# Attention scores with the memory keys stationary in 64x32 tiles and the queries moving, copied out and transposed back on TensorE

## The chip, the cores and the metric

The kernel runs on one core of a Trainium2 chip. The core has a matrix engine (PE, which loads a stationary operand, LDWEIGHTS, and then streams a moving operand through it, MATMUL), a vector engine (DVE), a scalar engine (ACT), a general engine (POOL) and a queue engine that issues the DMAs (SP). Matmul results land in PSUM and are read from there by DVE and ACT; everything else lies in SBUF. Each engine executes its own instructions in the order in which they were written and waits on semaphores for the others. The metric is the device time of one execution in microseconds.

## The reference

For each of 8 batches and 8 heads, 576 tokens of 64 dimensions are condensed into 32 memory slots, the tokens attend to the slots, and two feed-forward blocks follow:

```
a      = softmax over tokens of phi                 # [576, 32] per head
k_m    = a^T k ;  v_m = a^T v                       # [32, 64] per head
scores = q k_m^T / sqrt(64)                         # [576, 32] per head
attn   = softmax over the 32 slots of scores
x      = attn v_m                                   # heads side by side: [576, 512]
u      = x + (x^T U V)^T ;  y = u + relu(u w1) w2   # 512 -> 2048 -> 512
h      = relu(y w_in) ; gate the two halves, mix tokens with w_spatial ; out = gated w_out
```

The change is in the line `scores`.

## The kernel before

A generator, `att(b)`, prepares the attention of batch b while the matrix products of batch b-1 run: its pieces end in `yield`, and the product phases call it piece by piece. Batch 0 has a routine of its own (`first`), which the change leaves as it is, so the changed code runs 7 times, for batches 1 to 7. For batch 1 it is interleaved with the products of batch 0 (`mm<-gw,w2r` in f32 at L794), for batch 2 with the f16 products at L854, and for batches 3 to 7 with those of `st_phase` (L899, L910, L933), five times in the same order. Where the code is not inside a manual schedule, a scheduler places each instruction by its own model; the PE queue then holds what it holds in that order.

In `att` the steps around the change are: the condensed keys and values `nkv` (L592), two PE transposes of them into `tps` (L598), the copies out of `tps` (L601 by ACT for the keys, L606 by DVE for the values), a scale by way of `absmax`, `bmax_a` and `bmax_b` (the last one a small matmul at L159), and then the scores in three groups of token tiles, (0, 1), (2, 3) and (4,), of 128 tokens each and 64 in the last. For each group there is a bank of PSUM `sps`. Per token tile four matmuls (L629) hold 128 tokens of a pair of heads of `q` stationary and stream 64 columns of `kmt`, a block-diagonal tile of the keys of both heads (its other half is zero from the start). Each matmul of f32 operands is shown in the trace as two LDWEIGHTS and two MATMULs. DVE takes the maximum over the 32 slots (L633) and subtracts it (L636), ACT takes the exponential (L638), and in the next piece DVE sums and divides (L642 to L646), and ACT and DVE split the result into two f16 halves `ahl` (L650, L651). All of `ahl` is then multiplied with `u3h` (L660, ten matmuls, the last two on token tile 4).

The queries come in by `load_q` (L277): token tile s lies in one of two buffers `qt`, so tile s+2 can be loaded only once the scores of tile s have been computed. The SP queue issues these loads in order with all others. Token tile 4 of batches 3 to 7 is loaded early into a piece of `gw`. PSUM tiles named `at` share three banks, `mm` tiles five. `tmp` tiles share five buffers.

Of the kernel before, what the change touches and what calls it, by code (L numbers as in the profile page):

```python
# [12 lines left out]
ACTF = mybir.ActivationFunctionType  # L13
# [17 lines left out]
def mixer_kernel(  # L31
# [34 lines left out]
    def t1k():  # L66
        return tp.tile([128, 256], F32, tag="t1k", name="t1k", bufs=2)
# [81 lines left out]
    def bmax_a(am, n=128):  # L149
        e = tiny(1, I32)  # L150
        dve.tensor_single_scalar(e[:n], am[:n].bitcast(I32), EXP_MASK, op=ALU.bitwise_and)
        dg = tp.tile([128, 128], BF16, tag="dgb", name="dgb", bufs=3)
        dve.tensor_scalar(out=dg[:n, :n], in0=identb[:n, :n], scalar1=e[:n].bitcast(F32),
                          scalar2=None, op0=ALU.mult)
        return dg
# [112 lines left out]
    def rows(s):  # L268
        return 128 if s < 4 else 64
# [279 lines left out]
    def att(b):  # L549
# [46 lines left out]
        tps = at_tile()  # L596
        for g in range(2):
            pe.transpose(tps[:, g * 128:(g + 1) * 128], nkv[:, g * 128:(g + 1) * 128], ident)  # L598
        for e_ in range(2):
            r0 = slice(64 * e_, 64 * e_ + 64)  # L600
            act.activation(kmt[r0, :, e_, :],  # L601
                           tps[r0, e_ * 128:(e_ + 1) * 128].rearrange("p (q m) -> p q m", m=M), func=ACTF.Copy)
        vmt32 = a["vmt32"] = t1k()[:, 0:128]
        for e_ in range(2):
            r0 = slice(64 - 64 * e_, 128 - 64 * e_)
            dve.tensor_copy(vmt32[r0], tps[r0, e_ * 128:(e_ + 1) * 128])  # L606
        av = tiny()
        absmax(av, vmt32)
        dg = bmax_a(av)
        yield  # L610
        yield
        mv, rv, sv = sc[:, 4:5], sc[:, 5:6], sc[:, 6:7]
        bmax_b(dg, mv)
# [5 lines left out]
                                 op0=ALU.mult, op1=ALU.subtract)  # L619
        ahl = tp.tile([128, NST, 2, 256], F16, tag="pa", name="ahl")  # L620
        pool.memset(ahl[64:128, 4], 0.0)
        for grp in ((0, 1), (2, 3), (4,)):
            r = rows(grp[0])
            n = len(grp)
            sps = at_tile()
            for i, s in enumerate(grp):
                o4 = sps[:r, i * 256:(i + 1) * 256].rearrange("p (e q m) -> p e q m", e=2, m=M)
                for p in range(4):
                    pe.matmul(o4[:, :, p, :], a["q"][s][:, p, :r], kmt[:, p], start=True, stop=True)  # L629
                load_q(b, s + 2)  # L630
            sv3 = sps[:r, 0:n * 256].rearrange("p (h m) -> p h m", m=M)
            mxs = tiny(16)
            dve.tensor_reduce(out=mxs[:r, :n * 8], in_=sv3, axis=AX.X, op=ALU.max)  # L633
# [3 lines left out]
                              in1=mxs[:r, :n * 8].unsqueeze(2).to_broadcast([r, n * 8, M]), op=ALU.subtract)  # L637
            act.activation(ex[:r, 0:n * 256], ex[:r, 0:n * 256], func=ACTF.Exp, scale=0.125)  # L638
            yield
            yield  # L640
            sm = tiny(16)
            dve.tensor_reduce(out=sm[:r, :n * 8], in_=ex3, axis=AX.X, op=ALU.add)  # L642
# [1076 lines left out]
```

## Time and profile before

| | us |
|---|---|
| median of 3 runs | 1139.64 (1138.35 to 1140.41) |
| the profiled execution | 1138.26 |
| its span, first to last instruction | 1136.5 |
| PE busy | 1119.4 (98%) |
| DVE busy | 843.1 (74%) |
| ACT busy | 609.3 (54%) |
| L629, 280 records of score matmuls, busy | 32.2 (28.8 + 3.4) |

The span leaves 1.8 us of the execution outside it. An instruction is named by line, engine, operation and `output<-inputs`; a duration of PE is the time from entering to leaving the array, so that neighbours overlap, and what a group of matmuls costs is read from where the next group starts. "Idle before" is time in which the engine had nothing running, with the engine and tile that ended it.

### The profile page before, as it was taken

To read this page: it belongs to the slowest core of one execution; us is meant where nothing else is said; L and a number is where in the kernel's file an instruction comes from. 1 tells how busy PE (TensorE), PEld (TensorE's weight loads), DVE (VectorE), ACT (ScalarE), POOL (GpSimd) and SP (SyncE) were. 2 spreads that over 40 slices of the span, in tenths; PEclk is the share of its full clock that TensorE was granted. 3 is DMA by queue.
4 is the path that set the end of the run, shared out by engine and by line. 5 is a ranking of instruction groups with operands and counts; after the bars stand their busy time and mean duration, and the time that the engine had idled before them with its cause. 6 is when DMAs were issued, how large, how long until landed. Compare 5 with 4: busy or idle time off the path is not lost.

```text
span 1136.5 us, 28937 instructions
## 1 busy us (share of the span) xinstructions
PE 1119.4 (98%) x12015; PEld 884.4 (78%) x12015; DVE 843.1 (74%) x2217; ACT 609.3 (54%) x1308; POOL 90.5 (8%) x316
## 2 busy tenths in 40 slices
PE   8899999999999999999999999999999999999998
PEld 6566776777667997789867997779967898679966
DVE  6767688878786786868776787867868687866854
ACT  4768765746446354564365454563555543653543
POOL 3101011000010001100010000100011000100000
PEclk9999999999999999999999999999999999999999
DMA  9869741341526231441316213261304303130201
GB/s 357 315 259 348 263 173 59 117 147 39 184 79 208 72 127 42 151 147 60 146 59 218 87 36 148 93 206 60 144 25 157 125 20 128 44 111 2 110 19 43
DMA packets 54852, 145.69 MB, mean 128 GB/s; under 512 B 7808, under 2 KB 37248, under 8 KB 43584
## 3 DMA queue, kind: packets, MB, share of 16 engines
q1 hardware_dynamic: 54208, 143.16, 35.8%
q8 instruction: 94, 1.54, 0.6%
q10 hardware_dynamic: 512, 0.67, 0.2%
q14 instruction: 38, 0.31, 0.1%
HBM read 120.32 MB, written 23.49 MB: 127 GB/s over the span
## 4 chain that ended last, share of the span: by engine, by line
PE 85%; DVE 7%; ACT 4%; DMA 2%; issue 1%; POOL 1%; ACTq 0%; POOLq 0%; DVEq 0%
PE mm L899 23%; PE mm L933 13%; PE mm L1198 10%; PE mm L1228 8%; PE mm L1157 6%; PE mm L1086 5%; PE mm L794 4%; PE at L629 2%; PE mm L854 2%; PE at L735 2%; PE at L578 2%; PE mm L771 1%; PE mm L817 1%; PE mm L910 1%; DMA wsr<-w2d 1%
## 5 line engine op out<-in xcount | busy, mean ns | idle before, releaser
L899 PE MATMUL mm<-gw,w2r 128*128 128x144 f16 x2304 | 168.8, 226 | 0.0
L899 PEld LDWEIGHTS <-w2r 128*128 128x128 f16 x2304 | 152.4, 98 | 5.0
L933 PE MATMUL mm<-apr,z 128*128 128x288 f16 x1152 | 155.1, 286 | 0.0
L933 PEld LDWEIGHTS <-z 128*128 128x128 f16 x1152 | 109.7, 98 | 28.3 <-issue 2.0
L899 PE MATMUL mm<-gw,wa 128*128 128x144 f16 x1728 | 127.9, 226 | 0.0
L937 ACT ACTIVATE wsr<-mm 128x288 f32<-128x288 f32 x192 | 78.3, 408 | 86.2 <-DVE gw L921 42.8
L1198 PE MATMUL mm<-wsr,gw 128*128 128x288 f16 x896 | 114.3, 286 | 1.7 <-ACT gw L1161 1.6
L899 PEld LDWEIGHTS <-wa 128*128 128x128 f16 x1728 | 111.3, 98 | 3.5 <-issue 1.0
L1198 PEld LDWEIGHTS <-gw 128*128 128x128 f16 x896 | 85.6, 98 | 32.1 <-issue 9.7
L1157 PE MATMUL mm<-yhl,gw 128*128 128x288 f16 x768 | 99.4, 286 | 0.0
L1228 PE MATMUL mm<-ghl,wa 128*128 128x288 f16 x768 | 97.8, 286 | 0.0
L1228 PEld LDWEIGHTS <-wa 128*128 128x128 f16 x768 | 74.4, 98 | 22.8 <-issue 3.8
L1157 PEld LDWEIGHTS <-gw 128*128 128x128 f16 x768 | 73.4, 98 | 18.6 <-issue 0.6
L939 DVE TENSOR_TENSOR wsr<-wsr 128x288 f32<-128x288 f32 x96 | 44.0, 458 | 56.7 <-ACT wsr L937 56.7
L1086 PE MATMUL mm<-gw,yhl 128*128 128x512 f16 x384 | 85.5, 379 | 0.0
L921 DVE TENSOR_TENSOR gw<-wsr,gw 128x720 f16<-128x720 f32 x96 | 85.5, 900 | 0.0
L1213 ACT ACTIVATE ghl<-gw,ysc 128x288 f16<-128x288 f32 x64 | 34.2, 535 | 83.2 <-DVE gw L1212 83.2
L920 ACT ACTIVATE gw<-wsr 128x720 f16<-128x720 f32 x96 | 76.4, 796 | 0.5
L1086 PEld LDWEIGHTS <-yhl 128*128 128x128 f16 x384 | 37.0, 98 | 41.7
L794 PE MATMUL mm<-gw,w2r 128*128 128x288 f32 x256 | 65.9, 409 | 0.0
L1092 DVE BATCH_NORM_STATS2 tiny<-tmp 128x6 f32<-128x512 f32 (+1 forms) x40 | 25.6, 639 | 46.9 <-ACT tmp L1090 46.8
L794 PEld LDWEIGHTS mm<-gw,w2r 128*128 128x128 f32 x256 | 47.5, 190 | 15.1 <-issue 1.5
(309 smaller groups left out, 1867.2 us busy)
## 6 DMA issues: line engine op xcount, KB each, us to landing
wa<-w1d SPq DMA_DIRECT2D x22, 1024.0 KB, 5.0
kvt<-in_kv_dram SPq DMA_DIRECT2D x28, 516.0 KB, 5.0
gw<-wid SPq DMA_DIRECT2D x12, 1024.0 KB, 7.4
wsr<-wsd SPq DMA_DIRECT2D x7, 1440.0 KB, 6.3
out_dram<-tmp SPq DMA_DIRECT2D x64, 144.0 KB, 2.3
qt<-in_qT_dram SPq DMA_DIRECT2D x28, 256.0 KB, 3.7
gw<-in_w_dram SPq DMA_DIRECT2D x6, 1024.0 KB, 8.2
wa<-wod SPq DMA_DIRECT2D x6, 1024.0 KB, 4.8
```

The source lines that it names most:

```text
L794: pe.matmul(ps, w2r[:, f, d * 128:(d + 1) * 128], AT[0]["g"][:, f, :], start=False, stop=(f == 15))
L899: pe.matmul(ps[:, dd * QH:(dd + 1) * QH], w(c, dd, 1 - x), gs[:, m, c, y, :], start=(first and c == 0 and dd == 0 and i == 0), stop=(end a ...
L920: act.activation(h, X[:, 3:8], func=ACTF.Copy)
L921: dve.tensor_tensor(out=gs[:, 2:7, c, 1, :], in0=X[:, 3:8], in1=h, op=ALU.subtract)
L933: pe.matmul(ps, a["z"][:, k, x, f * 128:(f + 1) * 128], a["apr"][:, k, y, sl], start=(i == 0), stop=(i == 5))
L937: act.activation(o, pair(ps), func=ACTF.Relu, scale=CG)
L939: dve.tensor_tensor(out=X[:, 4:6], in0=X[:, 2:4], in1=X[:, 1:3], op=ALU.subtract)
L1086: pe.matmul(ps, yhl[:, k, x, s * 128:(s + 1) * 128], wih[:, k, 0, 1 - y, :], start=(i == 0), stop=(i == 11))
L1157: pe.matmul(ps, wih[:, k, 1, 1 - x, d * 128:(d + 1) * 128], a["yhl"][:, k, y, sl], start=(i == 0), stop=(i == 11))
L1198: pe.matmul(pss[d], vn[:, s, x if s < 4 else 0, ds], wsh[:, s, th, 1 - y, :], start=(s == 0 and i == 0), stop=(s == 4 and i == 1))
L1213: act.activation(ghl[:, d, 0, sl], u2, func=ACTF.Identity, scale=sgt)
L1228: pe.matmul(ps, (wo0 if b else woh)[:, k, 1 - x, d * 128:(d + 1) * 128], a["ghl"][:, k, y, sl], start=(i == 0), stop=(i == 11))
```

## The change

For each pair of heads the keys now lie plain in `kT` (64 rows of one head, 32 columns a pair), stationary, and the 128 tokens of `q` move. Eight matmuls per token tile, one for each head, go to eight different 64x32 tiles of the array (row half by `e_`, column quarter by `p`) and write two PSUM tiles, one for each `e_`, of 128 partitions (4 heads by 32 slots) by tokens. Two ACT copies bring them into a `tmp` tile `sT`, and PE transposes give the old layout back in `sps`. The matmuls of a group stand one or more pieces ahead of the transposes.

```diff
--- before.py
+++ after.py
@@ -596,18 +596,38 @@
         tps = at_tile()
         for g in range(2):
             pe.transpose(tps[:, g * 128:(g + 1) * 128], nkv[:, g * 128:(g + 1) * 128], ident)
+        vk = t1k()
+        vmt32, kT = vk[:, 0:128], vk[:, 128:256]
+        a["vmt32"] = vmt32
         for e_ in range(2):
             r0 = slice(64 * e_, 64 * e_ + 64)
-            act.activation(kmt[r0, :, e_, :],
-                           tps[r0, e_ * 128:(e_ + 1) * 128].rearrange("p (q m) -> p q m", m=M), func=ACTF.Copy)
-        vmt32 = a["vmt32"] = t1k()[:, 0:128]
+            act.activation(kT[r0], tps[r0, e_ * 128:(e_ + 1) * 128], func=ACTF.Copy)
         for e_ in range(2):
             r0 = slice(64 - 64 * e_, 128 - 64 * e_)
             dve.tensor_copy(vmt32[r0], tps[r0, e_ * 128:(e_ + 1) * 128])
         av = tiny()
         absmax(av, vmt32)
         dg = bmax_a(av)
+        G = ((0, 1), (2, 3), (4,))
+        sT = {}
+
+        def scores(i):
+            r = rows(G[i][0])
+            n = r * len(G[i])
+            ps = [at_tile() for e_ in range(2)]
+            for k, s in enumerate(G[i]):
+                for p in range(4):
+                    for e_ in range(2):
+                        r0 = slice(64 * e_, 64 * e_ + 64)
+                        pe.matmul(ps[e_][32 * p:32 * p + 32, k * r:(k + 1) * r], kT[r0, 32 * p:32 * p + 32],
+                                  a["q"][s][r0, p, :r], start=True, stop=True)
+                load_q(b, s + 2)
+            sT[i] = tmp()
+            for e_ in range(2):
+                act.activation(sT[i][:, e_ * 256:e_ * 256 + n], ps[e_][:, 0:n], func=ACTF.Copy)
+
         yield
+        scores(0)
         yield
         mv, rv, sv = sc[:, 4:5], sc[:, 5:6], sc[:, 6:7]
         bmax_b(dg, mv)
@@ -619,15 +639,14 @@
                                  op0=ALU.mult, op1=ALU.subtract)
         ahl = tp.tile([128, NST, 2, 256], F16, tag="pa", name="ahl")
         pool.memset(ahl[64:128, 4], 0.0)
-        for grp in ((0, 1), (2, 3), (4,)):
+        for gi, grp in enumerate(G):
             r = rows(grp[0])
             n = len(grp)
             sps = at_tile()
-            for i, s in enumerate(grp):
-                o4 = sps[:r, i * 256:(i + 1) * 256].rearrange("p (e q m) -> p e q m", e=2, m=M)
-                for p in range(4):
-                    pe.matmul(o4[:, :, p, :], a["q"][s][:, p, :r], kmt[:, p], start=True, stop=True)
-                load_q(b, s + 2)
+            for k in range(n):
+                for e_ in range(2):
+                    pe.transpose(sps[:r, k * 256 + e_ * 128:k * 256 + e_ * 128 + 128],
+                                 sT[gi][:, e_ * 256 + k * r:e_ * 256 + (k + 1) * r], ident)
             sv3 = sps[:r, 0:n * 256].rearrange("p (h m) -> p h m", m=M)
             mxs = tiny(16)
             dve.tensor_reduce(out=mxs[:r, :n * 8], in_=sv3, axis=AX.X, op=ALU.max)
@@ -637,6 +656,8 @@
                               in1=mxs[:r, :n * 8].unsqueeze(2).to_broadcast([r, n * 8, M]), op=ALU.subtract)
             act.activation(ex[:r, 0:n * 256], ex[:r, 0:n * 256], func=ACTF.Exp, scale=0.125)
             yield
+            if gi < 2:
+                scores(gi + 1)
             yield
             sm = tiny(16)
             dve.tensor_reduce(out=sm[:r, :n * 8], in_=ex3, axis=AX.X, op=ALU.add)
```

The SP queue for one of the five equal batches. `kvt`, `e`, `qt`, `phiT` are inputs of the attention, `wsr`, `gw` weights. Before:

```order
L259 DMA e<-in_phi_dram 64x256
L275 DMA kvt<-in_kv_dram 128x1032
L281 DMA qt<-in_qT_dram 128x4x128 x2
L131 DMA wsr<-wsd 128x5760
L128 DMA gw<-wid 128x4096
L281 DMA qt<-in_qT_dram 128x4x128 x2
L128 DMA gw<-wid 128x4096
```

The same stretch of SP now:

```order
L259 DMA e<-in_phi_dram 64x256
L275 DMA kvt<-in_kv_dram 128x1032
L281 DMA qt<-in_qT_dram 128x4x128 x4
L131 DMA wsr<-wsd 128x5760
L128 DMA gw<-wid 128x4096 x2
```

The first two `qt` are tiles 2 and 3 of this batch, released by the scores of tiles 0 and 1; the other two are tiles 0 and 1 of the next batch, released by the scores of tiles 2 and 3. These scores now stand a phase earlier, so all four loads follow one another.

The PE queue where the scores of batch 1 are computed (L794 now L815 is the f32 product of batch 0, L159 the small matmul of `bmax_b`). Before:

```order
L598 MATMUL at<-ident,nkv 128x128 x2
L794 MATMUL mm<-gw,w2r 128x288 x2
L629 MATMUL at<-kmt,qt 128x2x32 x8
L159 LDWEIGHTS onesb
L159 MATMUL mm<-dgb,onesb 128x128
L794 MATMUL mm<-gw,w2r 128x288 x17
L629 MATMUL at<-kmt,qt 128x2x32 x8
L794 MATMUL mm<-gw,w2r 128x288 x14
L629 MATMUL at<-kmt,qt 64x2x32 x4
```

The same stretch of PE now:

```order
L598 MATMUL at<-ident,nkv 128x128 x2
L815 MATMUL mm<-gw,w2r 128x288
L622 MATMUL at<-qt,t1k 32x128 x16
L815 MATMUL mm<-gw,w2r 128x288
L159 LDWEIGHTS onesb
L159 MATMUL mm<-dgb,onesb 128x128
L648 MATMUL at<-ident,tmp 128x128
L815 MATMUL mm<-gw,w2r 128x288
L648 MATMUL at<-ident,tmp 128x128 x3
L815 MATMUL mm<-gw,w2r 128x288 x3
L622 MATMUL at<-qt,t1k 32x128 x16
L815 MATMUL mm<-gw,w2r 128x288 x13
```

The first two groups of scores (L622) have moved close together: before, 17 products stood between them, now there are 5 and the transposes (L648). In the five equal batches 246 matmuls of L899 and 96 of L933 stood between the two groups; now there are, in this order, 12 of L899 (now L920), 24 of L910 (now L931), 6 of L920, L159, four transposes, and 12 of L920. The transposes of the second group, 12 of L920, the scores of token tile 4 (L622, 8 matmuls), 24 of L920 and their two transposes then stand where the second and third group of L629 stood before.

DVE at the end of the preparation, in the five equal batches (the second group's normalisation, then tile 4's; `y` belongs to the products). Before:

```order
L646 TENSOR_TENSOR tmp<-tmp,tinyw 128x512
L990 TENSOR_TENSOR y_6554<-mm,y_6554 128x2x144
L642 TENSOR_REDUCE tinyw<-tmp 64x8
L651 TENSOR_TENSOR ahl<-tmp,ahl 128x2x256
L165 TENSOR_REDUCE tiny<-y_6554 128x1
L643 TENSOR_SCALAR tinyw<-tinyw 64x8
L645 RECIPROCAL tinyw<-tinyw 64x8
L646 TENSOR_TENSOR tmp<-tmp,tinyw 64x256
L651 TENSOR_TENSOR ahl<-tmp,ahl 64x256
L995 TENSOR_TENSOR y_6554<-mm,y_6554 128x2x144
```

The same stretch of DVE now:

```order
L667 TENSOR_TENSOR tmp<-tmp,tinyw 128x512
L1011 TENSOR_TENSOR y_6689<-mm,y_6689 128x2x144
L663 TENSOR_REDUCE tinyw<-tmp 64x8
L672 TENSOR_TENSOR ahl<-tmp,ahl 128x2x256
L165 TENSOR_REDUCE tiny<-y_6689 128x1
L664 TENSOR_SCALAR tinyw<-tinyw 64x8
L666 RECIPROCAL tinyw<-tinyw 64x8
L667 TENSOR_TENSOR tmp<-tmp,tinyw 64x256
L1016 TENSOR_TENSOR y_6689<-mm,y_6689 128x2x144
L672 TENSOR_TENSOR ahl<-tmp,ahl 64x256
```

Only the last two have changed places; from L161 to here DVE's order is the same as before.

## Rows read from the trace of the kernel before

**Rows 1.** The page: busy time of each engine; granted clock in 40 slices.
```profile
PE 1119.4 (98%) x12015; PEld 884.4 (78%) x12015; DVE 843.1 (74%) x2217; ACT 609.3 (54%) x1308; POOL 90.5 (8%) x316
...
PEclk9999999999999999999999999999999999999999
```

**Rows 2.** The page: the chain that ended last, by engine.
```profile
PE 85%; DVE 7%; ACT 4%; DMA 2%; issue 1%; POOL 1%; ACTq 0%; POOLq 0%; DVEq 0%
```

**Rows 3.** Waits of PE: line, who ended it, us in total, times, longest.
```profile
PE at L629 <- DMA qt<-in_qT_dram: 0.2, 1, 0.2
```

**Rows 4.** Timeline of PE, batch 3, first scores: start, us, line, records.
```profile
383.21 0.38 PE L598 MATMUL at<-ident,nkv 128*128 128x128 f32 x2
383.43 1.66 PE L899 MATMUL mm<-gw,w2r 128*128 128x144 f16 x24
385.02 0.57 PE L910 MATMUL mm<-apr,vmu 64*64 64x144 f16 x24
385.52 0.55 PE L899 MATMUL mm<-gw,wa 128*128 128x144 f16 x6
...
385.96 1.95 PE L629 MATMUL at<-kmt,qt 128*128 128x64 f32 x16
387.75 0.91 PE L899 MATMUL mm<-gw,wa 128*128 128x144 f16 x12
```

**Rows 5.** Timeline of PE, two blocks of column tiles in f32, batches 0 and 1.
```profile
82.80 1.09 PE L758 MATMUL at<-wa,t1k 64*32 64x512 f32 x16
...
104.10 1.09 PE L578 MATMUL at<-kvt,e 128*32 128x129 f32 x32
```

**Rows 6.** Timeline of ACT, batch 3; in brackets idle time before and its end.
```profile
383.63 0.56 ACT L601 ACTIVATE kmt<-at 64x128 f32<-64x128 f32 x2 [4.68 <-PE at L598]
...
429.57 0.38 ACT L665 ACTIVATE pst<-at 128x256 f16<-128x256 f32 x1 [1.03 <-PE at L660]
```

**Rows 7.** Query loads after the scores of Rows 4: ns min/median/max, starts, landing.
```profile
L281 SPq DMA_DIRECT2D qt<-in_qT_dram x2: 566/572/578, 387.1 to 387.9; - x2
...
DMA to landing us min/median/max: 3.2/3.3/3.5
```

**Rows 8.** The landing of the same loads in batch 4.
```profile
DMA to landing us min/median/max: 3.3/3.8/4.4
```

**Rows 9.** Timeline of PE, batch 3, second and third group of scores.
```profile
415.75 0.22 PE L159 MATMUL mm<-dgb,onesb 128*128 128x128 bf16 x1
...
418.06 1.94 PE L629 MATMUL at<-kmt,qt 128*128 128x64 f32 x16
...
422.18 0.68 PE L629 MATMUL at<-kmt,gw 128*64 128x64 f32 x8
422.79 0.92 PE L899 MATMUL mm<-gw,w2r 128*128 128x144 f16 x12
...
428.94 0.60 PE L660 MATMUL at<-ahl,u3h 128*128 128x256 f16 x4
429.38 0.79 PE L899 MATMUL mm<-gw,w2r 128*128 128x144 f16 x10
```

**Rows 10.** Timeline of DVE in the same stretch of batch 3.
```profile
416.01 0.29 DVE L161 TENSOR_REDUCE tiny<-mm 128x1 f32<-128x128 f32 x1
...
418.84 1.37 DVE L1053 SCALAR_TENSOR_TENSOR yhl<-y,ysc,yhl 128x288 f16<-128x288 f32 x3
...
421.45 0.68 DVE L636 TENSOR_TENSOR tmp<-at,tinyw 128x512 f32<-128x512 f32 x1
...
428.58 0.42 DVE L651 TENSOR_TENSOR ahl<-tmp,ahl 64x256 f16<-64x256 f32 x1 [0.54 <-ACT ahl L650]
```

**Rows 11.** Timeline of PE, batch 2, first and second group of scores.
```profile
243.80 3.10 PE L854 MATMUL mm<-gw,w2r 128*128 128x288 f16 x24
246.74 1.00 PE L629 MATMUL at<-kmt,qt 128*128 128x64 f32 x8
247.98 1.10 PE L629 MATMUL at<-kmt,qt 128*128 128x64 f32 x8 [0.24 <-DMA qt<-in_qT_dram]
```

## The prediction

> **What bounds the kernel now.** I read the page first, then the chain, the waits of PE, and then timelines of the two places in a batch where the scores are computed. PE is busy 98% of the span, with the granted clock at nine tenths or more, its 2.4 GHz level, in every slice [rows 1], and 85% of the chain that ended last is PE work [rows 2]. Among PE's waits the scores have one entry, 0.2 us for a query load [rows 3]. So a microsecond taken out of PE's queue counts, as long as no other chain ends later at that place; and a wait put into it counts in full. I therefore price the PE work first and then look for what is late next.
>
> In batches 3 to 7 the order of the instructions is the same, so batch 3 stands for five. Times below are those of the profiled execution (1138.26 us, 1.38 below the median of 1139.64).
>
> **PE work, old and new.** A group of two token tiles costs PE from 385.96 to 387.75, 1.79 us for 16 records of 0.11 [rows 4]; the second group is alike, and tile 4 costs 0.61, with 0.09 of mode change ahead of it 0.70 [rows 9]. That is 4.28 us a batch.
>
> New, a group is 16 matmuls in eight 64x32 tiles, 32 records if each f32 matmul makes two as before. The trace has no such block with 128 columns. Two rows bound it. A block of eight 64x32 tiles in f32 with 512 columns shows 16 records in 1.09 us, so eight run at once, twice, some 0.45 us apart [rows 5]. The block of 32-column tiles with 129 columns, four at once, shows 32 records in 1.09 us; less the last one's 0.27 that is 0.82 for seven steps, 0.117 a step [rows 5]. Eight at once gives four steps of about 0.11 (512 columns in 0.45 scaled to 128 agrees), 0.44; four at once would give eight, 0.9. As lower end the f16 block L910 has six steps of four in 0.59 with entry and exit, against 0.0625 for a plain matmul, so about 0.06 a step: 0.25 for four [rows 4]. Entry and exit together are 0.59 less 6 x 0.0625, 0.22. I take 0.44 + 0.22 = 0.66, the row with the same tile shape and type (0.47 to 1.1). Tile 4 has half the columns: 0.14 + 0.22 = 0.36.
>
> A transposition: two of them hold PE from 383.21 to 383.43, 0.11 each, though each record lasts 0.27 [rows 4]. Four cost 0.44 a group; the two of tile 4 are 64 columns wide and need entry and exit like the old L629 there, 0.22 + 0.22. Sum: 2 x (0.66 + 0.44) + 0.36 + 0.44 = 3.00. Without waits PE saves 1.28 us a batch, 9.0 in seven.
>
> The Trainium skill, page "TensorE: Matmul & The Clock Gate", section "Part 4: PE-mode transpose", speaks against this: it gives about 275 ns for a transpose in a kernel and says that the clock's release does not come with transposes. Here the record's length agrees (0.27), but the next group starts after 0.11 and the clock stays whole [rows 1, 4]; by the page's figure, as an estimate, ten transposes would cost 2.75 instead of 1.1 us. Its result as a rival is below.
>
> **ACT copies.** Six a batch, two to a group. A copy of 128x256 out of PSUM takes 0.38, one of 64x128 takes 0.28 [rows 6], so 2 x 0.38 a group; bounds 0.28 and twice 0.38 each. They lie beside PE: ACT is idle 4.68 us ahead of L601 [rows 6]. They end about 1.5 us after the scores begin (0.65 until the last record has left the array, 0.76, and the handovers), and in batch 3 PE reaches the transposes after 2.8 us. Cost 0; the cover is 1.2 us.
>
> **The wait that the move adds: queries.** Tiles 2 and 3 go into the buffers of tiles 0 and 1. Before, PE came back for them 32 us later (385.96 to 418.06) [rows 4, 9]. Now, from the start of the first scores (call it A; 12 matmuls after the transposes of 383.43, so at 384.28): 0.55 until the next L920, 12 of them 0.75, L931 0.59, six 0.38, L159 0.06, four transposes 0.44, 12 of L920 0.75, entry 0.11: A+3.63. Tile 0 is free at A+0.45 (two steps and a record of 0.27), its load is issued at A+0.48 and lands 3.2 to 3.5 later [rows 7]: A+3.7 to A+4.0. The second issue follows the first by the 0.57 that an issue takes [rows 7], A+1.07, and lands at A+4.3 to A+4.6, while PE, done with tile 2, wants it at about A+4.05. PE thus stands 0.1 to 0.35 and then 0.3 to 0.55: S = 0.65 us. Bounds: 0 if the loads land half a microsecond sooner; about 1.5 if the second takes 4.4 as in batch 4 [rows 8]. Behind the waiting matmul all of PE's queue stands, so S counts in full. First stretch: 0.66 + 0.44 + 0.66 + S against 1.79, a change of S - 0.03.
>
> **What is late next: DVE.** In the second stretch PE gives up 1.79 + 0.70 and takes 0.44 + 0.36 + 0.44, a saving of 1.25. But L660 for tile 4, with all of PE behind it, needs the last `ahl`, and DVE works towards it nearly without a gap: L161 at 416.01 right after L159, then the products' L1053 until 420.21, L636 until 422.13, the last L651 until 429.00 [rows 10]. None of this begins sooner because the scores do: L1053 hangs on L159, and the order is kept. The last L660 started at 428.94 + 3 x 0.11 = 429.27 [rows 9]. So of 1.25 only 0.24 is to be had; the other 1.0 becomes a wait of L681 (the old L660) for DVE. The cover is thick: 1 us of dearer transposes in this stretch would cost nothing.
>
> Per batch 3 to 7: S - 0.03 - 0.24 = +0.38 us, five times +1.9.
>
> **Batches 1 and 2.** PE again saves 1.28, but between first and second scores only some 2 to 4 us remain. In batch 2, where before the scores stood 24 products apart, the load was already late by 0.24 [rows 11]; now twelve products (1.5 us) and the transposes lie between, and I reckon 1.4 us of waiting for the queries and 0.2 for the copies; in batch 1 likewise 0.8 and 0.7, the latter because one product is left between the steps. Sum 0 for both, bounds -1 and +1 each.
>
> Sum: 1138.26 + 1.9 = 1140.2; as a median, 1139.64 + 1.9 = **1141.5 us**. The change takes 9 us of work out of PE's queue and puts about 11 of waiting in.
>
> **Rivals.**
> Both waits fail to come: the loads land in time and DVE has room. Then 9.0 us are saved, 1130.6. For it: PE is the bound everywhere in the chain. Against: the landing times and DVE's 429.00 are rows.
> The queries land in time but DVE holds the end: 5 x -0.27 and some -0.8 in each of batches 1 and 2, 1136.7. For it: the margin on tile 2 is only 0.1 to 0.35.
> Slower, and more than forecast: two loads issued 0.6 apart share the queues and the second takes 4.4 as in batch 4 [rows 8]. S = 1.45, +1.2 a batch, 1147 with 1 us from batches 1 and 2. From S = 0.73 on the change is slower by more than 0.2%.
> Transposes in sequence at 0.27, as the page has it: in the second stretch hidden behind DVE, in the first +0.65, in batches 1 and 2 +1.65 each, so 1148. The two records of L598 in 0.38 speak against it [rows 4].
>
> **How the numbers follow.** A difference under 0.2% (2.3 us: 1137.4 to 1141.9) is what a measurement here cannot tell from none. Forecast 0.53, its own range 1139.5 to 1143.5, of which a good half lies under 1141.9; nothing late 0.06; DVE alone 0.15; late queries 0.20; slow transposes 0.06. Faster 0.06 + 0.09 = 0.15; same 0.06 + 0.32 = 0.38; slower 0.47. The range 1136.5 to 1146.5 leaves out nothing-late, slow transposes and the tails.
>
> **What would show it.** In the new profile: L622 waiting for DMA `qt` in every batch, some 0.6 us in batches 3 to 7; L681 waiting for DVE `ahl` about 1 us in each of these; transposes 0.11 apart; 32 records of L622 in about 0.7 us; no wait of L648 for ACT in batches 3 to 7. Wrong would be a span shorter by several us (then DVE's end moved, and I misread what L1053 hangs on), or waits of PE at L648.

## The result and the profile after

The changed kernel takes 1148.24 us (median of 6 runs, 1145.40 to 1153.36) against 1138.78 for the kernel before (6 runs): ratio 1.0086, 95% interval 1.0064 to 1.0109. It is about 9.5 us slower; forecast were 1141.5 us and 1.9 us slower. The profiled execution takes 1148.05 us with a span of 1146.1, 9.6 above that of before. Line numbers have moved: L629 is now L622 (scores) and L648 (transposes), L899 L920, L660 L681, L650 and L651 L671 and L672, L854 L875, L1053 L1074.

Busy time and clock, from the page (as [rows 1]), then the chain by engine (as [rows 2]):

```profile
PE 1114.4 (97%) x12365; PEld 867.6 (76%) x12365; DVE 844.5 (74%) x2217; ACT 620.0 (54%) x1350; POOL 89.5 (8%) x316
...
PEclk9999999999999999999999999999999999999999
...
PE 74%; DVE 11%; ACT 6%; DMA 5%; issue 2%; POOL 1%; SPq 0%; ACTq 0%; DVEq 0%; POOLq 0%
```

PE's share of the chain falls from 85 to 74%; what it loses goes to DVE, DMA and ACT. The waits of PE (line, who ended it, us in total, times, longest) name them, where [rows 3] had 0.2 us:

```profile
PE at L622 <- DMA qt<-in_qT_dram: 7.8, 10, 2.1
PE at L681 <- ACT ahl L671: 3.7, 5, 0.7
...
PE at L681 <- DVE ahl L672: 0.8, 5, 0.2
```

Where in a batch this falls is found with the same matmuls in both traces. From L598 on I count the product matmuls (those that write `mm`, without L159) and compare the times at which the 101st, the 283rd, the 601st and the next L598 start. In batches 3 to 7 these cuts make the first stretch (both L159 and scores around the first one), the z phase, the second stretch and the rest. Change against the kernel before in the profiled executions, us:

| | batch 1 | 2 | 3 | 4 | 5 | 6 | 7 |
|---|---|---|---|---|---|---|---|
| first stretch | | | +1.09 | +2.44 | +2.07 | +0.82 | +0.82 |
| z phase | | | 0.00 | 0.00 | +0.01 | 0.00 | 0.00 |
| second stretch | | | -0.22 | -0.22 | -0.23 | -0.22 | -0.23 |
| whole batch | +0.31 | +3.11 | +0.85 | +2.22 | +1.80 | +0.61 | +0.57 |

Their sum is 9.5 us, and 0.1 is lost ahead of batch 1. So two numbers are off from the forecast: the first stretch (0.6 forecast, 1.45 on the mean) and batch 2 (0 forecast, 3.11).

PE in batch 4, first stretch (start, us, line, records; idle before):

```profile
520.86 0.67 PE L622 MATMUL at<-qt,t1k 64*32 64x128 f32 x32
521.46 0.92 PE L920 MATMUL mm<-gw,w2r 128*128 128x144 f16 x12
...
523.25 0.61 PE L648 MATMUL at<-ident,tmp 128*128 128x128 f32 x4
523.69 0.91 PE L920 MATMUL mm<-gw,wa 128*128 128x144 f16 x12
524.80 0.45 PE L622 MATMUL at<-qt,t1k 64*32 64x128 f32 x16 [0.19 <-DMA qt<-in_qT_dram]
527.13 0.45 PE L622 MATMUL at<-qt,t1k 64*32 64x128 f32 x16 [1.88 <-DMA qt<-in_qT_dram]
```

The block of 32 records costs 0.60 (520.86 to 521.46) and four transposes 0.44 (523.25 to 523.69); then PE stands for tile 2 and, 1.88 us, for tile 3. The two loads behind it:

```profile
L281 SPq DMA_DIRECT2D qt<-in_qT_dram x2: 578/600/622, 521.4 to 522.0; - x2
...
DMA to landing us min/median/max: 3.3/4.2/5.0
```

The first lands after 3.3 us, the second after 5.0, where [rows 8] had 4.4 at most; in batch 5 it is 3.2 and 4.7, in batches 3, 6 and 7 3.2 to 3.7.

The second stretch of batch 3, PE and then DVE (as [rows 9, 10]):

```profile
422.67 0.60 PE L648 MATMUL at<-ident,tmp 128*128 128x128 f32 x4
...
423.95 0.34 PE L622 MATMUL at<-gw,t1k 64*32 64x64 f32 x16
424.23 1.67 PE L920 MATMUL mm<-gw,w2r 128*128 128x144 f16 x24
425.74 0.38 PE L648 MATMUL at<-ident,tmp 128*64 128x128 f32 x2
425.96 0.91 PE L920 MATMUL mm<-gw,w2r 128*128 128x144 f16 x12
...
433.21 0.28 PE L681 MATMUL at<-ahl,u3h 128*128 128x256 f16 x1 [0.74 <-ACT ahl L671]
433.66 0.27 PE L681 MATMUL at<-ahl,u3h 128*128 128x256 f16 x1 [0.16 <-DVE ahl L672]
```

```profile
421.26 0.16 DVE L174 RECIPROCAL ysc<-ysc 128x1 f32<-128x1 f32 x1 [0.34 <-POOL ysc L144]
422.65 0.52 DVE L1074 SCALAR_TENSOR_TENSOR yhl<-y,ysc,yhl 128x288 f16<-128x288 f32 x1 [1.23 <-ACT yhl L1073]
...
425.10 0.69 DVE L652 TENSOR_REDUCE tinyw<-at 128x16 f32<-128x512 f32 x1
...
433.19 0.42 DVE L672 TENSOR_TENSOR ahl<-tmp,ahl 64x256 f16<-64x256 f32 x1 [0.17 <-ACT ahl L671]
```

The transposes are done at 423.11, but DVE takes the maximum L652 at 425.10, after its `yhl`, and ends at 433.6; PE stands 0.74 + 0.16 for it (the 0.74 by way of ACT's L671, which had itself waited 2.23 us for DVE's L667). The 1.23 us in which DVE waits for ACT become important below.

Batch 2 (as [rows 11]), PE, then its busy time and granted clock by window (its length; busy time of PE, PEld, DVE, ACT and POOL with counts; the clock; DMA share and GB/s):

```profile
243.55 0.90 PE L875 MATMUL mm<-gw,w2r 128*128 128x288 f16 x6
246.60 0.68 PE L622 MATMUL at<-qt,t1k 64*32 64x128 f32 x16 [2.15 <-DMA qt<-in_qT_dram]
247.21 0.66 PE L875 MATMUL mm<-gw,w2r 128*128 128x288 f16 x2
247.81 0.68 PE L622 MATMUL at<-qt,t1k 64*32 64x128 f32 x16
248.42 2.82 PE L875 MATMUL mm<-gw,w2r 128*128 128x288 f16 x16
251.07 0.60 PE L648 MATMUL at<-ident,tmp 128*128 128x128 f32 x4
```

```profile
244.00:246.00 2.00, 0.45 (x4) 0.12 (x2) 2.00 (x6) 0.40 (x1) 0.37 (x2) 1.00 0.81 237
246.00:247.00 1.00, 0.40 (x16) 0.26 (x16) 0.31 (x1) 0.00 (x0) 0.00 (x0) 0.72 0.06 18
247.00:248.00 1.00, 1.00 (x25) 0.33 (x18) 0.00 (x0) 0.00 (x0) 0.00 (x0) 0.50 0.00 0
248.00:249.00 1.00, 1.00 (x19) 0.44 (x9) 0.00 (x0) 0.36 (x2) 0.00 (x0) 0.50 0.12 28
249.00:250.00 1.00, 1.00 (x7) 0.60 (x6) 0.16 (x1) 1.00 (x4) 0.00 (x0) 0.57 0.56 123
```

After PE stood 2.15 us for the query load, the granted clock is 0.50, the 1.2 GHz level, for some 3 us: the blocks take 0.60 each, and 16 products 2.65 (248.42 to 251.07) instead of 16 x 0.123. The page's row of 40 slices shows none of this. The Trainium skill tells of such a fall of the clock by waits for a DMA ("TensorE: Matmul & The Clock Gate", section "HAM oscillation — how this bites in real kernels"); here it came after 2.15 us of standing and not after the 1.88 and 1.59 us of batches 4 and 5. The length of the wait does not decide it alone: in the same trace PE stands 2.63 us ahead of an L159 at the end of batch 2 (until 326.42), and the clock stays at 1.00.

### The profile page after: what moved, and what is told of

The parts are those of the page before. It is cut to its first block, busy times and chain, and to the rows that moved or that the text cites. A ratio compares the mean times of both kernels' runs of the same rounds, so it can differ in the third digit from the quotient of the medians.

```text
span 1146.1 us, 29691 instructions
## 1 busy us (share of the span) xinstructions
PE 1114.4 (97%) x12365; PEld 867.6 (76%) x12365; DVE 844.5 (74%) x2217; ACT 620.0 (54%) x1350; POOL 89.5 (8%) x316
## 3 DMA queue, kind: packets, MB, share of 16 engines
q8 instruction: 96, 1.57, 0.6%
## 4 chain that ended last, share of the span: by engine, by line
PE 74%; DVE 11%; ACT 6%; DMA 5%; issue 2%; POOL 1%; SPq 0%; ACTq 0%; DVEq 0%; POOLq 0%
PE mm L920 17%; PE mm L954 13%; PE mm L1219 10%; PE mm L1249 8%; PE mm L1178 6%; PE mm L1107 5%; PE mm L815 3%; DMA qt<-in_qT_dram 2%; PE at L756 2%; PE at L578 2%; PE mm L792 1%; PE mm L875 1%; DMA q<-in_qT_dram 1%; PE mm L838 1%; DVE yhl L1074 1%
## 5 line engine op out<-in xcount | busy, mean ns | idle before, releaser
L920 PE MATMUL mm<-gw,w2r 128*128 128x144 f16 x2304 | 170.6, 226 | 0.0
L920 PEld LDWEIGHTS <-w2r 128*128 128x128 f16 x2304 | 152.6, 98 | 7.9 <-issue 2.7
L954 PE MATMUL mm<-apr,z 128*128 128x288 f16 x1152 | 155.1, 286 | 0.0
L954 PEld LDWEIGHTS <-z 128*128 128x128 f16 x1152 | 109.7, 98 | 28.3 <-issue 2.0
L920 PE MATMUL mm<-gw,wa 128*128 128x144 f16 x1728 | 128.8, 226 | 0.0
L920 PEld LDWEIGHTS <-wa 128*128 128x128 f16 x1728 | 111.1, 98 | 4.6 <-issue 2.0
L815 PE MATMUL mm<-gw,w2r 128*128 128x288 f32 x256 | 66.7, 409 | 0.0
L815 PEld LDWEIGHTS mm<-gw,w2r 128*128 128x128 f32 x256 | 47.3, 190 | 15.2 <-issue 2.1
```

The source lines that it names most:

```text
L815: pe.matmul(ps, w2r[:, f, d * 128:(d + 1) * 128], AT[0]["g"][:, f, :], start=False, stop=(f == 15))
L920: pe.matmul(ps[:, dd * QH:(dd + 1) * QH], w(c, dd, 1 - x), gs[:, m, c, y, :], start=(first and c == 0 and dd == 0 and i == 0), stop=(end a ...
L954: pe.matmul(ps, a["z"][:, k, x, f * 128:(f + 1) * 128], a["apr"][:, k, y, sl], start=(i == 0), stop=(i == 5))
```

## The experiments

Times stand against runs of the kernel before on the same chip. For each kernel the table gives the changes in batch 2 and, as means over batches 3 to 7, in the four parts, from one profile each (us).

| kernel | ratio, 95% interval | batch 2 | first | z | second | rest |
|---|---|---|---|---|---|---|
| the change | 1.0086 (1.0064 to 1.0109) | +3.11 | +1.45 | 0.00 | -0.22 | -0.02 |
| e1_q2 | 1.0014 (1.0002 to 1.0027) | +1.37 | +0.30 | 0.00 | -0.16 | -0.02 |
| e3_fill | 1.0070 (1.0056 to 1.0084) | +1.26 | +1.57 | 0.00 | -0.22 | -0.02 |
| e4_more | 1.0130 (1.0112 to 1.0147) | +4.15 | +1.51 | +2.12 | -2.27 | +1.20 |
| e5_tile | 1.0058 (1.0045 to 1.0070) | +0.77 | +0.47 | +0.58 | +0.42 | +0.09 |
| e6_move | 1.0075 (1.0062 to 1.0088) | +0.65 | +2.56 | +0.44 | -1.78 | -0.01 |
| e7_fix | 1.0004 (0.9993 to 1.0015) | +1.71 | +0.25 | 0.00 | -0.22 | -0.01 |
| e8_pool | 0.9994 (0.9984 to 1.0004) | +0.05 | +0.19 | 0.00 | -0.42 | -0.08 |
| e9_oldpool | 0.9993 (0.9984 to 1.0002) | +1.63 | 0.00 | 0.00 | 0.00 | -0.04 |
| e10_turn | 1.0076 (1.0062 to 1.0090) | +0.44 | +0.81 | +1.66 | -1.90 | +1.15 |
| e11_twice | 1.0001 (0.9989 to 1.0013) | +1.49 | +0.35 | 0.00 | -0.31 | +0.07 |
| e12_slot | 0.9941 (0.9926 to 0.9957) | +1.49 | +0.24 | 0.00 | -1.46 | -0.02 |
| e13_oldslot | 1.0001 (0.9989 to 1.0014) | +0.30 | 0.00 | 0.00 | 0.00 | -0.01 |

Batch 2's total is loose by some 1.7 us (e9_oldpool has the old code there and shows +1.63; e7_fix and e8_pool have the same code and show +1.71 and +0.05), so batch 2 is read by its rows; the parts of batches 3 to 7 repeat within 0.1 where no query is waited for. The traces name what makes it loose. At the end of batch 2 PE waits for DVE's `dgb` ahead of an L159, 2.36 to 2.65 us in all 14 profiles, that of the kernel before too. In five of them (e4_more, e7_fix, e9_oldpool, e11_twice, e12_slot) the granted clock is 0.50 for some 3 us behind this wait, in the other nine it stays at 1.00. First e7_fix, then e8_pool, PE and clock:

```profile
324.69 0.25 PE L159 MATMUL mm<-dgb,onesb 128*128 128x128 bf16 x1 [2.64 <-DVE dgb L153]
324.75 3.06 PE L1182 MATMUL mm<-yhl,gw 128*128 128x288 f16 x12
...
325.00:326.00 1.00, 1.00 (x6) 0.65 (x5) 0.83 (x6) 1.00 (x5) 0.00 (x0) 0.50 0.00 0
```

```profile
322.17 0.23 PE L159 MATMUL mm<-dgb,onesb 128*128 128x128 bf16 x1 [2.64 <-DVE dgb L153]
322.24 1.63 PE L1182 MATMUL mm<-yhl,gw 128*128 128x288 f16 x12
...
323.00:324.00 1.00, 1.00 (x16) 0.60 (x21) 0.85 (x5) 0.89 (x5) 0.00 (x0) 1.00 0.02 8
```

The same wait of 2.64 us is followed by 12 products in 3.06 us or in 1.63. Why the clock falls in one execution and not in another is not shown.

**e1_q2: the query of tile 2 early.**

```diff
+                t = AT[b]["q"][2] = gw[:, 8320:8832].rearrange("p (g c) -> p g c", g=4)
+                sp.dma_start(t, qT[b, :, :, 256:384])
```

> The changed kernel, with the queries of token tile 2 loaded a phase earlier into free space in gw for batches 3 to 7 (as token tile 4 already is); batches 1 and 2 are untouched. Theory 'late queries' (what the changed kernel loses in batches 3 to 7 is PE standing at L622 for the query loads of tiles 2 and 3, mostly the second of the two): the only load left between the two blocks is tile 3's, issued 0.5 us after the first scores begin, so the waits of L622 for qt in batches 3 to 7 (now 0.7, 2.1, 1.6, 0.4 and 0.3 us of PE standing and more in the weight loads) fall below 0.3 each, the first stretch of each batch costs what it cost before the change (change 0 to 0.2 instead of 0.8 to 2.4), and the time falls by 6 to 7 us to about 1142. Batch 2 still stands 2.1 us at L622. Rival 'dear tiles' (the 64x32 blocks with their mode changes and the transposes cost more than their records show): the time falls by less than 2 us and stays above 1146.

1141.69 us. The first stretch falls from +1.45 to +0.30 and the excess of five batches from 6.0 to 0.6 us, so the query waits were the loss there; tile 3's load is still late by 0.6 us in batch 3. It shows more, by chance: in batch 2, which it leaves untouched, its load came sooner.

```profile
246.68 0.45 PE L622 MATMUL at<-qt,t1k 64*32 64x128 f32 x16 [1.16 <-DMA qt<-in_qT_dram]
247.06 0.42 PE L875 MATMUL mm<-gw,w2r 128*128 128x288 f16 x2
247.52 0.45 PE L622 MATMUL at<-qt,t1k 64*32 64x128 f32 x16
247.90 2.13 PE L875 MATMUL mm<-gw,w2r 128*128 128x288 f16 x16
249.87 0.60 PE L648 MATMUL at<-ident,tmp 128*128 128x128 f32 x4
```

The clock stays at 1.00, and the same queue from the first block to L648 takes 3.19 us instead of 4.47 (246.60 to 251.07): the slow clock cost 1.28 us there.

**e3_fill: batch 2's wait filled with work.**

```diff
+            if b == 2 and i == 1:
+                for _ in range(28):
+                    pe.matmul(ps[0][:, 0:128], onesb, identb, start=True, stop=True)
```

> The changed kernel with 28 matmuls more in batch 2 alone, 128 columns of bf16 each, whose result is overwritten at once; they stand directly ahead of the second block of scores, where PE stands 2.15 us for a query load, and fill about 1.7 us of that. Theory 'clock' (the 2.15 us of standing make the granted clock fall from 1.00 to 0.50, and the 3.5 us that follow run at half speed, which costs batch 2 another 1.5 to 1.9 us on top of the wait): the granted clock stays at 1.00 through batch 2, the blocks of 16 records of L622 take 0.4 instead of 0.61 us and 16 products 2.0 instead of 2.65, the way from L598 to the next L159 behind the scores falls from 26.65 to about 25.0 us, and the kernel gets faster by 1.5 to 1.9 us though PE does more. Rival 'work' (the blocks are slow in batch 2 for another reason, such as two products only between them): the blocks stay at 0.61 and the way stays at 26.6 or grows by what the 28 matmuls add.

The granted clock is 1.00 in every window from 240 to 255, the 18 products behind the blocks take 2.21 us (0.123 each), and from L598 to L159 it is 25.2 us instead of the change's 26.65. PE did 1.7 us more and was through this stretch 1.5 us sooner, as the theory has it. That the filler kept the clock whole is likely but not shown: unfilled, the wait at this place was followed by the fall both times that it was so long (2.15 us here, 2.06 in e4_more), but the longer wait at L159 left the clock whole in nine profiles of 14, and there is one profile with the filler. In the time, 1148.57 us, this can't be seen: the interval overlaps that of the change, and in this profile batch 7 lost 2.4 us to a late query.

**e4_more: three more pieces in the first half.**

```diff
-every(2, lambda: nf[0] < 19 and step(nxt))
+every(2, lambda: nf[0] < 25 and step(nxt))
```

> The changed kernel, with three more pieces of the next batch's attention called in the first half of the phase of batches 3 to 7: the transposes, the softmax of the second group and the scores of tile 4 then stand some 29 us earlier, and only tile 4's softmax is left for the second stretch. Theory 'the DVE chain holds the end' (in the second stretch DVE, with ACT in the chain, ends at the last ahl, and L681 waits for it about 0.9 us in each of five batches, which swallows what PE saves there): the waits of L681 vanish (4.5 us in all now), and the time falls by about 4.5 us to 1143.5; it could fall by up to 5 if L681 also starts earlier. Rival 'PE waits anyway' (the stretch ends at something else, as the products' own yhl): the wait moves to another line and the time stays within 1.5 us of 1148. The query waits at L622 stay as they are in both.

1155.02 us, 11 more than expected. The second stretch did what the theory said, -2.27 instead of -0.22, and no wait of L681 is left. But the z phase takes 2.12 more: 0.72 for the transposes and the block that came in, and with them DVE's and ACT's work (in all PE waits 2.6 us for ACT at L954 and 2.0 for DVE at L920), and behind the second stretch PE now waits 1.2 a batch for the `dgb` of L153, since later pieces moved up too. I had not priced the place that the work goes to.

**e5_tile: tiles without the move.**

```diff
         yield
-        scores(0)
         yield
...
+            scores(gi)
             sps = at_tile()
...
             yield
-            if gi < 2:
-                scores(gi + 1)
             yield
```

> The change without its move: scores in 64x32 tiles, copied out and transposed back, but each group's scores stand where they stood before the change, directly ahead of its copies and transposes, so the query loads have their 32 us again in batches 3 to 7 and the transposes have 7 to 9 products between themselves and the scores. Theory 'the loss is the move' (tiles and transposes are as cheap as their records, 0.66 and 0.44 a group; the queries were made late by the move): no wait for qt in batches 3 to 7; the transposes wait some 0.4 to 0.6 us for the ACT copies in each group; first stretch 0.66 + 0.5 + 0.44 against 1.79, second stretch held by DVE; -0.5 us a batch in batches 3 to 7, 0 in batches 1 and 2: about 1136.5 (1135 to 1138), some 11 to 12 us below the changed kernel. Rival 'the loss is the tiling': slower than the kernel before, 1142 or more.

Neither theory held: the time is the rival's, its reason is not. The query waits are gone, but the kernel is 6.7 us slower than before, and the tiles are not dear either (0.60 a block, 0.44 the transposes). The wait is a third one:

```profile
PE at L648 <- ACT tmp L627: 7.1, 15, 0.7
```

The copies, which cost nothing in the changed kernel, are waited for when they have 7 to 9 products for cover: in batch 4 0.70, 0.24 and 0.48 us. So it is the distance that the move puts between scores and transposes that makes the tiles usable. Of the z phase's +0.58 the profile names 0.28 (L952 waits for ACT); the rest stays open.

**e6_move: the move without tiles.** On the kernel before:

```diff
         yield
+        scores(0)
         yield
...
-            sps = at_tile()
+            sps = sT[gi]
...
             yield
+            if gi < 2:
+                scores(gi + 1)
             yield
```

> The move without the tiles: the score matmuls of the kernel before (128 tokens stationary, straight into the layout that DVE reads, no copies and no transposes), but the matmuls of a group stand where the changed kernel has its score blocks, one or more pieces ahead of the softmax. Theory 'late queries and DVE at the end': in the first stretch of batches 3 to 7 the second group's 1.79 us come in and a wait for qt with them (tile 0 is free 0.9 us after the start, tile 1 after 1.8, the loads land 3.2 to 5.0 us later, PE is there after 4.2 and 5.2: 0.2 to 1.5), in the second stretch only 0.2 to 0.3 of the 1.79 that go out is kept, because DVE ends no sooner: +1.7 to +3 us a batch, +9 to +15 in five, some 1 to 2 in batch 2: ratio 1.009 to 1.014. Rival 'moved work costs nothing by itself': the 1.79 us come in and go out alike, only the wait is left, +0.2 to 1.5 a batch, ratio 1.001 to 1.007.

Ratio 1.0075. The first stretch is as expected (1.79 plus 0.4 to 1.2 of waiting), but the second gave back 1.78, as the rival had it, not 0.2 to 0.3. In DVE's queue the second group's softmax stands at the border of the first stretch and the z phase there (in batch 3 from the maximum at 393.97 to the last `ahl` at 400.2), and at the end only tile 4's is left. My DVE chain is a bound of the order in which the transposes come so late, not of the stretch.

**e7_fix: queries on time in batches 2 to 7.** On e1_q2:

```diff
-            if gi < 2:
+            late = b == 2 and gi == 0
+            if gi < 2 and not late:
                 scores(gi + 1)
...
             yield
+            if late:
+                scores(1)
+                yield
             yield
```

> As the run with token tile 2 loaded early for batches 3 to 7, and in batch 2 alone the second block of scores stands 12 products (1.5 us) later, with 12 products between it and its transposes. Theory: batch 2 lost 1.2 us there to the query load (2.15 in the changed kernel's profile), which is now hidden; no wait for qt is left anywhere but 0.5 in batch 1, the clock stays whole, and the time is 1 to 1.5 us under that run: level with the kernel before (ratio 0.999 to 1.001), although PE has about 9 us less to do. What PE saves in batches 3 to 7 stands as waits of L685 for ahl, 4 to 5 us in all. Rival: batch 2 is bound by what DVE and ACT have to do for w2r there, then the wait only changes its name and the time stays at ratio 1.0014.

1139.11 us, level with the kernel before, as expected. In batch 2 the 283rd product now comes 0.3 us sooner than before the change, instead of 2.8 later. Three waits of L622 for queries are left, 1.8 us in all, one of them 0.70 for tile 4 in batch 2, where 0.5 in batch 1 alone was expected. L685 (the old L681) still waits 4.5 us for `ahl`, and the second stretch keeps 0.22.

**e8_pool and e9_oldpool: 0.69 us off DVE.** One line, on e7_fix and on the kernel before:

```diff
-            dve.tensor_tensor(out=ahl[:r, s0:s0 + n, 1, :], ...
+            (pool if gi == 1 and b > 2 else dve).tensor_tensor(out=ahl[:r, s0:s0 + n, 1, :], ...
```

> As the run before in this list (queries on time in batches 2 to 7), and in batches 3 to 7 the low half of the second group's ahl (one subtraction of 128x512, 0.69 us on DVE, 16 us of 1440 ns kind on POOL by the nearest row of 128x512 there) is computed by POOL, beside DVE's work for tile 4. Theory 'the DVE chain holds the end': tile 4's last ahl comes 0.6 to 0.7 us sooner in each of five batches, the waits of L685 fall from about 0.9 to 0.3 a batch, and the time falls by 3 to 3.5 us against the run before, to ratio 0.997: faster than the kernel before. Rival 'POOL is too slow': L685 waits for POOL's half instead, and the time is the same within 1 us.

> The kernel before the change with the same subtraction on POOL in batches 3 to 7. Theory: there PE is the one that ends last in that stretch (its last matmuls on ahl start 0.00 to 0.3 us after DVE's end without a wait), so giving DVE 0.69 us less saves 0 to 0.3 us a batch, in all under 1.5 us (ratio 0.9987 to 1.000); that is the difference to the run with the same edit on the changed kernel. Rival 'DVE bounds both': the same 3 to 3.5 us are saved here, ratio 0.997.

e8_pool gained 0.2 a batch, not 0.6 to 0.7, and not because POOL was late. DVE of e8_pool in batch 3, then POOL:

```profile
426.37 0.72 DVE L665 TENSOR_SCALAR tinyw<-tinyw 64x8 f32<-64x8 f32 x1
427.12 0.20 DVE L667 RECIPROCAL tinyw<-tinyw 64x8 f32<-64x8 f32 x1
```

```profile
425.91 1.16 POOL L673 TENSOR_TENSOR ahl<-tmp,ahl 128x512 f16<-128x512 f32 x1 [8.54 <-ACT ahl L672]
```

L665 takes 0.15 to 0.18 elsewhere; here it ends at 427.09, 0.02 after POOL's subtraction, and so it is in all five batches. The 0.69 taken from DVE came back as 0.56 of standing still. This agrees with the Trainium skill, "SBUF — State Buffer", section "SBUF: two separate sides": DVE, in some kinds of instruction, and GpSimd share a port pair that one of them holds for a whole instruction. Not every DVE instruction was held: the reduction L165 of 0.73 us, whose last 0.5 us lie beside the same subtraction, took no longer than without it.

e9_oldpool came out in time as expected, but it is no test of the old kernel: DVE's L643 is held there in the same way (0.71 to 0.72 us in all five batches), so DVE got only some 0.1 us out of the edit. That test is e13_oldslot, below.

**e10_turn: the transposes of the second group into the first stretch.** On e7_fix (`turn` holds the transposes of a group):

```diff
+            sps = back.pop(gi, None) or turn(gi)
...
+            if b > 2 and gi == 0:
+                back[1] = turn(1)
             yield
...
-every(2, lambda: nf[0] < 19 and step(nxt))
+every(2, lambda: nf[0] < 21 and step(nxt))
```

> The changed kernel with the queries on time in batches 2 to 7 (token tile 2 loaded early in batches 3 to 7, the second block of batch 2 twelve products later), and in batches 3 to 7 the transposes of the second group stand one piece ahead of their softmax, in the first stretch, 24 products behind their scores; the first half of the phase calls one piece more for that. The run with the move alone gained all of the 1.78 us that it took out of the second stretch, because DVE took up the second group's maximum as soon as its scores lay in PSUM, before the z phase, and had only tile 4 left at the end. Theory 'what DVE holds at the end is the second group's softmax, and it hangs on the transposes': second stretch -1.5 to -1.8 us a batch instead of -0.2, first stretch +0.45 for the transposes that move in, z phase +0.2 to +0.6 for DVE's work there; -0.6 a batch against the run with all queries on time, about 3 us in five batches: ratio 0.9965 to 0.998, faster than the kernel before. Rival 'the z phase has no room' (in the run with three more pieces it took 2.0 us a batch and the maximum behind it 1.1 more): first +0.45, z phase +1.5 or more, ratio 1.000 or above.

The rival held: second stretch -1.90, z phase +1.66, behind it +1.15, ratio 1.0076. Moved there, DVE's 3 us make PE wait as in e4_more; in e6_move they cost only 0.44, perhaps because PE's old scores had lengthened the first stretch; no run tests this.

**e11_twice: transposes of the second stretch done twice.** On e7_fix:

```diff
-            for k in range(n):
+            for k in [k for _ in range(2 if gi and b > 2 else 1) for k in range(n)]:
```

> As the run with all queries on time in batches 2 to 7, and in batches 3 to 7 the transposes of the second group and of tile 4 are done twice (six more of 0.11 us a batch, the same values written again). Theory 'the DVE chain holds the end of the second stretch': the wait of L685 for ahl shrinks by 0.4 to 0.66 a batch, the second stretch stays at -0.2 us against the kernel before, at most 0.2 of the first four's 0.44 is seen because they put off DVE's maximum: 0 to +1 us in five batches, ratio 1.000 to 1.001. Rival 'PE work counts there': +0.66 a batch, +3.3 us, ratio 1.003 and a second stretch of +0.4.

Ratio 1.0001, second stretch -0.31. Six more transposes a batch, 0.66 us of PE, cost nothing: the wait of L685 fell from 4.5 to 0.8 us.

**e12_slot and e13_oldslot: the second group's transposes (in e13, the old scores) directly ahead of the second stretch's L159.** On e7_fix and on the kernel before; the first half prepares as many pieces as there, the second stretch begins with one more, and one empty piece is added for what follows:

```diff
+            if b > 2 and gi == 0:
+                back[1] = turn(1)
             yield
...
             def late():
+                if early.pop() if early else False:
+                    step(nxt)
                 if next(yf, "end") == "end":
```

> The changed kernel with the queries on time in batches 2 to 7, and in batches 3 to 7 the transposes of the second group stand directly ahead of the L159 of the second stretch, 36 products earlier than in the changed kernel and behind the z phase, where the run before put them ahead of it. After that L159 DVE stands idle 0.34 and 1.23 us, for POOL and for ACT, before its first product of yhl; the second group's maximum and subtraction (0.68 and 0.68) now stand in its queue ahead of that. Theory 'DVE's chain holds the end, and it has a gap that only lacked its input': the last ahl comes 0.7 to 1.2 us sooner, the waits of L696 for ahl (0.9 a batch) vanish or fall under 0.3, second stretch -0.9 to -1.2 instead of -0.2, nothing in the z phase and nothing behind: 3.5 to 5 us in five batches against the run with all queries on time, ratio 0.996 to 0.998: faster than both kernels. Rival: the maximum stands ahead of L161 and puts the scale of y off by 0.7 us, and with it the yhl that the products wait for, or L159 waits for DVE's dgb behind the stretch as in the two runs that called more pieces (+1.1 a batch): ratio 1.000 or above.

> The kernel before the change, with the same reordering as the run before: in batches 3 to 7 the second group of its old score matmuls stands directly ahead of the L159 of the second stretch, and DVE takes up its maximum there. It tells whether the 6.8 us of that run come from the reordering alone. Theory: in the kernel before PE, not DVE, ends last in that stretch, so DVE's earlier end saves nothing: 0 to -0.3 us a batch, ratio 0.9985 to 1.0005. Rival 'the order alone is the gain': second stretch -1 us or more here too, ratio 0.996 or less.

e12_slot takes 1133.67 us, ratio 0.9941 (0.9926 to 0.9957): faster than both kernels, more than expected. Its DVE and PE in batch 3:

```profile
420.49 0.69 DVE L659 TENSOR_REDUCE tinyw<-at 128x16 f32<-128x512 f32 x1 [0.38 <-PE at L636]
421.10 0.28 DVE L161 TENSOR_REDUCE tiny<-mm 128x1 f32<-128x128 f32 x1
421.30 0.68 DVE L662 TENSOR_TENSOR tmp<-at,tinyw 128x512 f32<-128x512 f32 x1
...
423.39 1.79 DVE L1089 SCALAR_TENSOR_TENSOR yhl<-y,ysc,yhl 128x288 f16<-128x288 f32 x4
```

```profile
431.20 0.54 PE L935 MATMUL mm<-gw,w2r 128*128 128x144 f16 x6
431.58 0.60 PE L696 MATMUL at<-ahl,u3h 128*128 128x256 f16 x4
```

Maximum and subtraction now fill the time in which DVE waited for POOL and ACT, and the last four L696 run without a gap. The second stretch gains 1.46 of the 1.55 that PE gave up there (1.79 + 0.70 less 0.44 + 0.28 + 0.22), and five batches 6.2 us in all. The same order on the old scores gains nothing (1.0001), though DVE is through sooner there as well: in batch 3 its last `ahl` ends at 429.17 and the last four matmuls on `ahl` begin at 430.23, where before the change it was 429.00 and 428.94. It takes both, less work on PE and a DVE that is through sooner.

## Why the prediction was wrong

- **PE work**: right in kind, too dear in size. A block costs 0.60 (forecast 0.66), four transposes 0.44 (0.44), tile 4's block 0.28 (0.36) and its transposes 0.22 (0.44): 2 x 1.04 + 0.50 = 2.58 a batch, a saving of 1.70 instead of 1.28. The rival of slow transposes is out: they are 0.11 apart. The Trainium skill ("TensorE: Matmul & The Clock Gate", section "Part 4: PE-mode transpose") gives about 275 ns for one; here that is the length of a record and not the step from one to the next.
- **ACT copies at no cost**: right in batches 3 to 7; e5_tile shows the price without the cover, 0.2 to 0.7 us a group.
- **The query wait S, forecast 0.65, is the step that failed in batches 3 to 7.** Without waits the first stretch would be 0.60 + 0.44 + 0.60 - 1.79 = -0.15; it is +1.45, so S is 1.6. Order, issue times and PE's arrival were within 0.1 of the forecast (3.7 us after A); the second of two loads issued 0.6 us apart lands after 4.7 and 5.0 us in two batches of five, and I had taken 3.2 to 3.5 with 4.4 as an exception. In these two S is 2.6 and 2.2. In the other three, with landings of 3.4 to 3.7, it is still 1.0 to 1.2: the rows name 0.3 to 0.7 of standing, and the block of the second group comes in two halves of 0.39, one for each load, where the sum had one of 0.60; the rest is in no row. On the mean it is the rival "late queries" (S = 1.45) that came, in part by luck, since it had 1.45 in each batch. e1_q2 shows the price by taking the wait away. The rival's reason, two loads that share the queues, is not shown: loads issued equally close landed in time in other batches, and why some are late stays open.
- **DVE at the end of the second stretch**: right, -0.22 against -0.24, and its cover of 1 us as well (e11_twice). "None of this begins sooner" was true of the changed kernel, but no bound of the work: e12_slot gets 1.46. "Nearly without a gap" misread the trace of before, where DVE stands 0.34 for POOL and 1.23 for ACT between L161 and the first L1053, the room that e12_slot uses:

```profile
418.04 0.52 DVE L1053 SCALAR_TENSOR_TENSOR yhl<-y,ysc,yhl 128x288 f16<-128x288 f32 x1 [1.23 <-ACT yhl L1052]
```

- **Batch 2, forecast 0 with bounds of 1, is the other step that failed**: +3.11. The wait was 2.15 (1.4 forecast, the loads landed after 4.3 and 4.4), and the working had no term for what a wait does to the clock: 1.28 us more. The longer wait (0.75) and the clock make 2.0 of the 3.1. The rows name 0.46 more, PE at L875 waiting for DVE's `w2r`, which the working did not have; the rest stays open. Batch 1, +0.31, was inside its bounds.
- **Sum**: five batches +6.0 instead of +1.9, batch 2 +3.1 instead of 0, batch 1 +0.3. The likeliest case rested on the usual landing time, and the rival, whose row stood in the trace, was given 0.20. The rival's sum for the five batches agrees (+1.2 a batch), but for batches 1 and 2 it had +1, not +3.4.

## What to carry to other kernels

Price a wait for a DMA that follows another closely by the slowest landing in the trace, not by the median; and where it keeps PE standing for 2 us or so, as here, reckon with a fall of the clock behind it as a risk (1.3 us here): it came in some executions and not in others. Where two engines end close together, work taken from one is worth only what the other leaves: ask which of the late engine's inputs could stand ready in a gap that it already has, and move the input there, not the work to a phase that looks idle.

## What the runs showed of the hardware

- Waits of 2.15 and 2.06 us on PE (batch 2 of the change and of e4_more) were followed by about 3 us at a granted clock of 0.50; waits of 1.16 (same place), 1.59 and 1.88 us left it at 1.00, and with 28 small matmuls in the wait it stayed at 1.00 in the one profile of e3_fill. A wait of 2.36 to 2.65 us in each of 14 profiles was followed by a clock of 0.50 in five and of 1.00 in nine.
- A DVE operation of 0.15 us that met a 1.16 us subtraction of POOL lasted 0.72 and ended with it, in all ten batches of e8_pool and e9_oldpool; a reduction of 0.73 us beside the same subtraction was not held.
- Eight 64x32 tiles in f32 with 128 columns: 32 records in 0.60 us with entry and exit, 16 records of 64 columns in 0.28.
- Of two 256 KB loads issued 0.6 us apart the second landed after 3.4, 3.4, 3.7, 4.7 and 5.0 us in five batches of the change; in e3_fill and e4_more, with the same loads, after 3.4 to 5.0.
